# Banded attention and a gated feed-forward network on one core: another order for the loads, the transposes and the first feed-forward tile

## The chip, the core and the metric

The kernel runs on one core of a Trainium2 chip. Its engines run side by side, each through its own list of instructions in a fixed order: TensorE (PE, with its weight loads as PEld), VectorE (DVE), ScalarE (ACT), GpSimd (POOL) and SyncE (SP). The metric is the device time of one execution in microseconds (us); the time given is the median of the runs shown. An execution taken with the profiler gives the trace.

## The reference

Inputs q, k and v have 8 batches, 8 heads, 576 positions and 64 channels per head. Heads 0 to 3 use a plain window, heads 4 to 7 a dilated one:

```python
rel = pos[:, None] - pos[None, :]
mask_plain = (rel >= 0) & (rel < 32)
mask_dil   = (rel >= 0) & (rel < 128) & (rel % 4 == 0)
scores = where(mask, q @ k.T / 8, -1e9)
attn   = softmax(scores) @ v
x      = attn, heads side by side          # 4608 tokens x 512
out    = (((x @ w1) * (x @ w2)) @ w3) @ w_out   # w1, w2: 512x1024; w3: 1024x1024; w_out: 1024x512
```

## The kernel before, in words

**Attention.** The work of one batch is four steps: for each half of the positions (`hf`, 288 positions) one for the plain heads (`u` = 0) and one for the dilated heads (`u` = 1). A step computes scores on TensorE in two parts (L250), exponentials on ScalarE (L262), the product with a mask on VectorE (L264), the products with V on TensorE (L287), a reciprocal and a scaling on VectorE (L297, L298), and transposes into the channel-major activation `XT` (`to_channels`, L311 and L318), copied by VectorE for `u` = 0 (L326) and by ScalarE for `u` = 1 (L328). The operands come from `qn` and `kn` by transposes on VectorE (`transpose_qk`: into `qt` at L223, into `kt` at L212 or L223), V for the plain heads straight from memory (`vp`), and V for the dilated heads from a staging tile `vst` that a copy spreads into `vd` (`spread_vd`, two copies, L139). In the names of buffers qt0 and kt0 stand for `u` = 0, qt1 and kt1 for `u` = 1.

**Feed-forward.** w3 and w_out are first multiplied into one matrix `wf` (`fuse_t`, `fuse_m`). Tokens are taken in 9 tiles of 512. `ffn1` computes one block of 128 columns of x@w1 and x@w2 (two groups of four matmuls, L394), copies the first to SBUF on ScalarE (L404) and multiplies the second by it on VectorE (L405) into `gt`. Three PSUM banks `f` serve these groups in turn, so the third group ahead waits for the product before it. `ffn2` multiplies by `wf` (L429). Tile 0 is computed in two parts, tokens 0 to 287 and 288 to 511, since the first part needs only the first half of batch 0.

**Order.** Everything is issued by one hand-written sequence. The attention is a list of small pieces, `phases`; the feed-forward calls `point()` before each group, and a table `marks` says how many phases must have been issued by which point. Phases up to `done_at[1]` come before the first feed-forward group. `done_at[n]` is the place in the list at which step n has reached `XT`; the steps of batch b are 4b to 4b + 3. Inside the list the spread of V and the transposes for the next batch stand between the steps of the batch before it.

**Loads.** All loads are issued by GpSimd in program order, eight at most under way: the ninth issue waits for the first to land, and so on. They convert from float32 to bfloat16 on the way. The order is: batch 0 (q, k, vp, vst), w1 and w2, batch 1, w_out, w3 in four pieces, then batches 2 to 7, each issued by `prefetch` in the middle of the steps two batches ahead of it.

Of the kernel before, what the change touches and what calls it, by code (L numbers as in the profile page):

```python
# [22 lines left out]
HALF = 288  # L23
# [4 lines left out]
TB = 512  # L28
# [6 lines left out]
def kernel(  # L35
# [11 lines left out]
    nc = tc.nc  # L47
    B, H, s_, d_ = q.shape
# [5 lines left out]
    KFF = d_ff // P  # L54
# [47 lines left out]
    def load_qk(b, split=False):  # L102
        for nm, dst, src in (("qn", qn, q), ("kn", kn, k)):
            dst[b] = qk_pool.tile([P, 2, ROWS * D], BF16, tag=nm, name=nm)
        for u in range(2) if split else (slice(0, 2),):
            for dst, src in ((qn, q), (kn, k)):
                x = src[b].rearrange("(u h) (j a) d -> (h j) u (a d)", u=2, a=ROWS)
                nc.gpsimd.dma_start(out=dst[b][:, u], in_=x[:, u])  # L108

    def load_vp(b):  # L110
        vp = vps[b % NV]
        base = v[b, 0]

        def rows(p0, n, j0, nj):
            return bass.AP(
                tensor=base.tensor,
                offset=base.offset + (96 * j0 - 32 + p0) * D,
                ap=[[D, n], [96 * D, nj], [1, D]],
            )

        if b == 0:
            nc.gpsimd.dma_start(out=vp[32:P, 0:1, 0:D], in_=rows(32, 96, 0, 1))
            nc.gpsimd.dma_start(out=vp[:, 1:24, 0:D], in_=rows(0, P, 1, 23))
        else:
            nc.gpsimd.dma_start(out=vp[:, :, 0:D], in_=rows(0, P, 0, 24))

    def load_vd(b):
        vst[b] = qk_pool.tile([P, 2, 4, 4 * D], BF16, tag="vst", name="vst")
        for w in range(2):
            nc.gpsimd.dma_start(  # L130
                out=vst[b][:, w, :, :],
                in_=v[b, 4:8, 64 * w : 64 * w + 512, :].rearrange(
                    "h (p r) d -> p h (r d)", r=4
                ),
            )

    def spread_vd(b):
        for w in range(2):
            nc.vector.tensor_copy(  # L139
                out=vds[b % 2][:, w, :, 0:D],  # L140
                in_=vst[b][:, w, :, :].rearrange("p h (r d) -> p (h r) d", r=4),
            )
# [37 lines left out]
    def const_pool():  # L180
        def keep(t, base, pattern, cm):
            nc.gpsimd.affine_select(
                out=t, in_=t, compare_op=AL.is_ge, fill=0.0,
                base=base, pattern=pattern, channel_multiplier=cm,
            )

        mp = mp0.rearrange("p (r i) -> p r i", r=4)
        keep(mp, 32, [[1, 4], [4, 24]], -1)
        keep(mp, -1, [[-1, 4], [-4, 24]], 1)
        keep(md0, 0, [[56, 2], [1, RES]], -1)  # L190
        keep(md0, 31, [[-56, 2], [-1, RES]], 1)
        make_identity(nc, ident, nomemset=True)
# [12 lines left out]
    def transpose_qk(b, u, which):  # L205


        src, dst = ((qn, qts), (kn, kts))[which]
        t = src[b][:, u, :].bitcast(U32).rearrange("p (a i) -> p a i", a=ROWS)
        o = dst[u][b % 2].rearrange("p s c -> p (s c)").bitcast(U32)  # L210
        if u == 0 and which == 1:
            nc.vector.transpose(  # L212
                out=o[:, PADK : PADK + S].rearrange("p (j a) -> p a j", a=ROWS), in_=t
            )
            return
        for odd in range(2):
            n = 5 - odd
            step = (2 * 144 + 4, 5 - 2 * 144)[odd]
            first = o[:, 2 * 144 * odd : 2 * 144 * odd + 1]
            pitch = first.ap[0]  # L220
            for a1 in range(2):
                a0 = 2 * odd + a1
                nc.vector.transpose(  # L223
                    out=bass.AP(
                        tensor=first.tensor,
                        offset=first.offset + 144 * a1,
                        ap=[pitch, [1, n], [9, 16], [step, 2]],
                    ),
                    in_=t[:, a0 : a0 + 4 * n - 3 : 4, :],
                )  # L230

    class Step:
# [98 lines left out]

    early = [True]
    steps = [
        Step(4 * b + 2 * hf + u, b, u, hf)
        for b in range(B)
        for hf in range(2)
        for u in range(2)
    ]
    phases, done_at = [], {}
    issued = {0, 1}  # L340

    def prefetch(b):
        if b < B and b not in issued:
            issued.add(b)
            load_qk(b)
            load_vp(b)
            load_vd(b)

    def s_tile(hp):
        return ps_e if early[0] and hp else ps_s  # L350

    for i in range(len(steps) + 2):
        st = steps[i] if i < len(steps) else None
        p1 = steps[i - 1] if 1 <= i <= len(steps) else None
        p2 = steps[i - 2] if i >= 2 else None
        at = i % 4
        b = i // 4
        if st is not None and at == 0:
            phases.append(lambda b=b: transpose_qk(b, 1, 0))
        if at == 2 and b + 1 < B and st is not None:  # L360
            phases.append(lambda b=b: (spread_vd(b + 1), transpose_qk(b + 1, 0, 0)))
        if at == 3 and b + 1 < B and st is not None:
            phases.append(lambda b=b: transpose_qk(b + 1, 0, 1))
        if st is not None:
            phases.append(lambda st=st: st.scores(0, s_tile(0)))
        if p2 is not None:
            phases.append(lambda st=p2: st.to_channels())
            done_at[i - 2] = len(phases)
        if p1 is not None:
            phases.append(lambda st=p1: st.values(0))  # L370
        if st is not None and at == 0:
            phases.append(lambda b=b: transpose_qk(b, 1, 1))
            if b == 0:
                phases.append(lambda: spread_vd(0))
        if st is not None:
            phases.append(lambda st=st: st.scores(1, s_tile(1)))
        if p1 is not None and p1.u == 1:
            phases.append(lambda st=p1: st.values(1))
        if st is not None and at == 1:
            phases.append(lambda b=b: prefetch(b + 2))  # L380


    gts = {}
# [95 lines left out]
    load_wo()
    for g in range(4):  # L480
        load_w3(g)

    transpose_qk(0, 0, 0)
    transpose_qk(0, 0, 1)
    const_spread()
    n0 = done_at[1]
    for ph in phases[:n0]:
        ph()
# [2 lines left out]

    marks = [(0, n0), (14, done_at[3]), (29, done_at[7]), (69, done_at[11])]
    for t in range(3, 8):
        marks.append((72 + 24 * (t - 2) - 3, done_at[4 * t + 3]))
    xs, ys = [m[0] for m in marks], [m[1] for m in marks]
# [6 lines left out]
            phases[state[1]]()  # L504
            state[1] += 1

    for f in range(KFF):
        ffn1(0, f, point, 0, HALF)
    for f in range(KFF):
        ffn1(0, f, point, HALF, TB)  # L510
    for f in range(KFF):
        ffn1(1, f, point)
    fuse_t(0)
# [44 lines left out]
```

## Time and profile before

| | |
|---|---|
| median of the 3 runs shown | 322.04 us (319.61 to 322.6) |
| the profiled execution, its own time | 322.75 us |
| span in its trace | 321.1 us |
| TensorE busy in the span | 266.6 us (83%) |
| VectorE busy | 182.7 us (57%) |
| ScalarE busy | 122.0 us (38%) |
| GpSimd busy | 44.6 us (14%) |

The busy shares are means over the whole span. Idle time of an engine is given with what ended it; a number at a row's start is a time in us from the start of the span.

### The profile page before, as it was taken

The numbers are of one execution on the slowest core, as the hardware profiler recorded it, in microseconds if no ns is written. First come the engines' busy times: TensorE is split into PE (matmuls) and PEld (weight loads), VectorE is DVE, ScalarE is ACT, GpSimd is POOL, SyncE is SP. The second block draws the span as 40 slices with busy tenths as digits, with TensorE's granted clock in tenths as the row PEclk, the third lists the DMA queues.
The fourth block names the chain that finished last, engine by engine and source line by source line (L and its number), as shares of the span: only waits on it lengthen the run. The fifth ranks groups of instructions, "written<-read, shape, count | busy, mean of one in ns | idle before, by whom it ended". The sixth has DMA issues, their size and how long they took to land.

```text
span 321.1 us, 6289 instructions
## 1 busy us (share of the span) xinstructions
PE 266.6 (83%) x2586; PEld 144.1 (45%) x2624; DVE 182.7 (57%) x401; ACT 122.0 (38%) x205; POOL 44.6 (14%) x61
## 2 busy tenths in 40 slices
PE   0230089567997989999999999999999999999994
PEld 0130057445643545554545555545554554444441
DVE  4530388489674546478787787877775453132210
ACT  1220035324435343454535444454453542323332
POOL 8741414102200004000400400000000000000000
PEclk9999999859899899999999999999999999999999
DMA  7999999995910044923991892111111112111124
GB/s 121 176 210 198 200 212 209 192 181 82 169 22 2 0 77 69 205 80 54 167 145 34 143 191 63 35 35 44 56 35 33 35 46 55 47 53 56 44 65 131
DMA packets 47645, 31.86 MB, mean 99 GB/s; under 512 B 26624, under 2 KB 37888, under 8 KB 47616
## 3 DMA queue, kind: packets, MB, share of 16 engines
q0 software_dynamic: 41760, 22.02, 52.0%
q1 hardware_dynamic: 5856, 9.44, 10.0%
q8 instruction: 20, 0.33, 0.4%
q14 instruction: 9, 0.07, 0.1%
HBM read 44.03 MB, written 9.44 MB: 167 GB/s over the span
## 4 chain that ended last, share of the span: by engine, by line
PE 73%; DMA 16%; DVE 3%; POOL 3%; issue 1%; ACT 1%; POOLq 0%; ACTq 0%
PE f L394 36%; PE f L429 20%; DMA w3n<-in_moe_w_dram 7%; PE ps_s L250 6%; DMA vst<-in_v_dram 6%; PE f L459 5%; DMA w_sb<-in_moe_w_dram 4%; PE ps_o L287 4%; PE ps_x L318 1%; PE ps_x L445 1%; PE ps_x L311 1%; ACT w3T L451 1%; DVE xo L298 1%; DVE qt L223 1%; POOL vst L130 0%
## 5 line engine op out<-in xcount | busy, mean ns | idle before, releaser
L394 PE MATMUL f<-XT,w_sb 128*128 128x512 bf16 (+2 forms) x617 | 144.0, 366 | 1.3 <-issue 0.3
L394 PEld LDWEIGHTS <-w_sb 128*128 128x128 bf16 x640 | 57.7, 100 | 50.2
L405 DVE TENSOR_TENSOR gt<-f,asb 128x512 bf16<-128x512 f32 (+2 forms) x80 | 50.5, 631 | 42.6 <-PE f L394 38.7
L429 PE MATMUL f<-wf_sb,gt 128*128 128x512 bf16 x277 | 68.1, 380 | 0.6
L262 ACT ACTIVATE et<-ps_s 128x576 bf16<-128x576 f32 x61 | 39.8, 653 | 65.6 <-PE ps_s L250 65.4
L404 ACT CAST asb<-f 128x512 bf16<-128x512 f32 (+2 forms) x80 | 43.4, 542 | 51.8 <-PE f L394 50.6
L437 ACT COPY osb<-f 128x512 f32<-128x512 f32 x36 | 21.1, 585 | 53.8 <-PE f L429 50.4
L287 PEld LDWEIGHTS <-et 128*128 128x128 bf16 x448 | 21.9, 104 | 40.1 <-issue 28.3
L250 PE MATMUL ps_s<-qt,kt 32*128 32x72 bf16 (+1 forms) x856 | 29.0, 206 | 12.4 <-DVE kt L212 8.6
L429 PEld LDWEIGHTS <-gt 128*128 128x128 bf16 x288 | 25.8, 98 | 27.9
L298 DVE TENSOR_TENSOR xo<-ps_o,rcp 72x512 bf16<-72x512 f32 (+1 forms) x48 | 37.2, 775 | 1.7
L250 PEld LDWEIGHTS <-kt 32*128 32x128 bf16 x896 | 21.0, 99 | 35.3 <-issue 19.1
L287 PE MATMUL ps_o<-vd,et 128*128 128x65 bf16 x256 | 13.6, 198 | 26.8 <-DVE xo L298 26.8
L223 DVE STREAM_TRANSPOSE qt<-qn 128x160 uint32<-128x160 uint32 (+1 forms) x64 | 24.6, 422 | 4.5 <-DMA qn<-in_q_dram 3.4
L264 DVE TENSOR_TENSOR et<-et,mask_di 128x576 bf16<-128x576 bf16 x32 | 14.5, 455 | 15.3 <-ACT et L262 14.3
L264 DVE TENSOR_TENSOR et<-et,mask_pl 128x576 bf16<-128x576 bf16 x32 | 14.3, 447 | 12.8 <-ACT et L262 12.8
L139 DVE COPY vd<-vst 128x1024 bf16<-128x1024 bf16 x16 | 6.5, 434 | 25.1 <-DMA vst<-in_v_dram 25.1
L297 DVE RECIPROCAL rcp<-ps_o 72x8 f32<-72x8 f32 (+1 forms) x48 | 9.9, 207 | 18.4 <-PE ps_o L287 17.8
L108 POOL DMA_DIRECT2D qn<-in_q_dram x9 | 6.2, 687 | 93.0 <-DVE qt L223 43.1
L459 PE MATMUL f<-wo_sb,w3T 128*128 128x512 bf16 x60 | 16.6, 405 | 0.2
L287 PE MATMUL ps_o<-vp,et 128*128 128x65 bf16 x192 | 10.4, 209 | 4.1 <-DVE et L264 3.3
L130 POOL DMA_DIRECT2D vst<-in_v_dram x16 | 12.1, 762 | 7.3 <-DVE xo L298 3.4
(41 smaller groups left out, 130.5 us busy)
## 6 DMA issues: line engine op xcount, KB each, us to landing
out_dram<-osb SPq DMA_DIRECT2D x32, 144.0 KB
vst<-in_v_dram POOLq DMA_DIRECT2D x16, 256.0 KB, 9.9
qn<-in_q_dram POOLq DMA_DIRECT2D x7, 576.0 KB, 8.2
kn<-in_k_dram POOLq DMA_DIRECT2D x7, 576.0 KB, 7.2
vp<-in_v_dram POOLq DMA_DIRECT2D x7, 384.0 KB, 9.4
w3n<-in_moe_w_dram POOLq DMA_DIRECT2D x4, 512.0 KB, 20.4
w_sb<-in_moe_w_dram POOLq DMA_DIRECT2D x2, 768.0 KB, 14.2
wo_sb<-in_moe_w_out_dram POOLq DMA_DIRECT2D x1, 1024.0 KB, 23.0
```

The source lines that it names most:

```text
L223: nc.vector.transpose(out=bass.AP(tensor=first.tensor, offset=first.offset + 144 * a1, ap=[pitch, [1, n], [9, 16], [step, 2]],), in_=t[:, ...
L250: nc.tensor.matmul(out=sp[:, g, i * nq : (i + 1) * nq], lhsT=kt[prt, k0 : k0 + P, c], rhs=rhs[:, q0 : q0 + nq, c] if u else rhs.rearrange( ...
L262: nc.scalar.activation(out=ev, in_=sp[:, :, 0:HALF], func=ACT.Exp, scale=scale)
L264: nc.vector.tensor_tensor(out=ev, in0=ev, in1=mk.unsqueeze(1).to_broadcast([P, 2, HALF]), op=AL.mult)
L287: nc.tensor.matmul(out=ps_o[:, hp, j * (D + 1) : (j + 1) * (D + 1)], lhsT=self.et[:, c0 : c0 + P], rhs=rhs, start=True, stop=True,)
L298: nc.vector.tensor_tensor(out=xo[0:nq, :, 0:j, :], in0=ov[:, :, :, 0:D], in1=rcp[0:nq, :, 0:j].unsqueeze(3).to_broadcast([nq, 2, j, D]), o ...
L394: nc.tensor.matmul(out=ps, lhsT=w_sb[:, c, f * P : (f + 1) * P], rhs=XT[:, c, t0 + lo : t0 + hi], start=(c == 0), stop=(c == DCH - 1),)
L404: nc.scalar.copy(out=a_sb[:, 0 : hi - lo], in_=ps)
L405: nc.vector.tensor_tensor(out=gts[t][:, f, lo:hi], in0=pss[1], in1=a_sb[:, 0 : hi - lo], op=AL.mult)
L429: nc.tensor.matmul(out=y, lhsT=gts[t][:, f, tb * P : (tb + 1) * P], rhs=wf_sb[:, f, :], start=(f == 0), stop=(f == KFF - 1),)
L437: nc.scalar.copy(out=o_sb, in_=y)
L459: nc.tensor.matmul(out=ps, lhsT=w3T[ft][:, g, :], rhs=wo_sb[:, g, :], start=(g == 0), stop=(g == KFF - 1),)
```

## The change

The order of the loads, of the attention steps and of the first feed-forward tile is rewritten. The instructions are the same, but for where the first spread of V runs and how the first loads of w1 and w2 are cut.

- Steps of `u` = 1 come before steps of `u` = 0 in each half, and the transposes follow that order: for the next batch the `u` = 1 transposes stand between the steps of the batch before, and its `u` = 0 transposes at its own first step. The spread of the next batch moves from the third step (ahead of the q transposes) to the fourth (behind the k transposes).
- The phases of batch 0 are a list of their own; nothing of batch 1 stands in it. Batch 1 starts with its `u` = 1 transposes and its spread.
- vst is loaded ahead of vp. w1 and w2 are loaded in halves of 512 columns, the first half ahead of batch 1, the second behind it.
- The feed-forward of tile 0 goes by four blocks at a time: both parts of the tokens for blocks 0 to 3, then for blocks 4 to 7.
- The spread of batch 0 is done by ScalarE.

```diff
 def load_qk(b, split=False):
-        for u in range(2) if split else (slice(0, 2),):
+        for u in (1, 0) if split else (slice(0, 2),):
...
 def spread_vd(b):
         for w in range(2):
-            nc.vector.tensor_copy(
+            copy = nc.vector.tensor_copy if b else nc.scalar.copy
+            copy(
                 out=vds[b % 2][:, w, :, 0:D],
...
     steps = [
-        Step(4 * b + 2 * hf + u, b, u, hf)
+        Step(4 * b + 2 * hf + 1 - u, b, u, hf)
         for b in range(B)
         for hf in range(2)
-        for u in range(2)
+        for u in (1, 0)
     ]
...
-        if st is not None and at == 0:
-            phases.append(lambda b=b: transpose_qk(b, 1, 0))
-        if at == 2 and b + 1 < B and st is not None:
-            phases.append(lambda b=b: (spread_vd(b + 1), transpose_qk(b + 1, 0, 0)))
-        if at == 3 and b + 1 < B and st is not None:
-            phases.append(lambda b=b: transpose_qk(b + 1, 0, 1))
...
+    def segment(lo, hi):
+        for i in range(lo, hi + 2):
...
+            if i == lo:
+                phases.append(lambda b=b: transpose_qk(b, 1, 0))
+                phases.append(lambda b=b: transpose_qk(b, 1, 1))
+                if lo:
+                    phases.append(lambda b=b: spread_vd(b))
+            if st is not None:
+                if at == 0:
+                    phases.append(lambda b=b: transpose_qk(b, 0, 0))
+                if at == 2 and 4 * (b + 1) < hi:
+                    phases.append(lambda b=b: transpose_qk(b + 1, 1, 0))
+                if at == 3 and 4 * (b + 1) < hi:
+                    phases.append(lambda b=b: transpose_qk(b + 1, 1, 1))
+                phases.append(lambda st=st: st.scores(0, s_tile(0)))
...
+                if at == 3 and 4 * (b + 1) < hi:
+                    phases.append(lambda b=b: spread_vd(b + 1))
...
+    segment(0, 4)
+    segment(4, 4 * B)
...
-    marks = [(0, n0), (14, done_at[3]), (29, done_at[7]), (69, done_at[11])]
+    marks = [(0, n0), (8, done_at[3]), (16, done_at[3]), (30, done_at[7]), (69, done_at[11])]
...
-    for f in range(KFF):
-        ffn1(0, f, point, 0, HALF)
-    for f in range(KFF):
-        ffn1(0, f, point, HALF, TB)
+    for f4 in range(0, KFF, 4):
+        for lo, hi in ((0, HALF), (HALF, TB)):
+            for f in range(f4, f4 + 4):
+                ffn1(0, f, point, lo, hi)
```

What this does to the order on three engines:

GpSimd's issues from the first batch's last loads on, before (a row `x2` is two loads; `vst_134` is batch 0; `qn_141`, `kn_142`, `vp1_84` and `vst_146` are batch 1):

```order
L130 DMA vst_134<-in_v_dram 128x4x256 x2
L146 DMA w1_sb_75<-in_moe_w1_dram 128x4x256
L146 DMA w2_sb_76<-in_moe_w2_dram 128x4x256
L146 DMA w1_sb_75<-in_moe_w1_dram 128x4x768
L146 DMA w2_sb_76<-in_moe_w2_dram 128x4x768
L108 DMA qn_141<-in_q_dram 128x2x1152
L108 DMA kn_142<-in_k_dram 128x2x1152
L125 DMA vp1_84<-in_v_dram 128x24x64
L130 DMA vst_146<-in_v_dram 128x4x256 x2
L152 DMA wo_sb_77<-in_moe_w_out_dram 128x8x512
```

and now (`vst_132` and `vp0_83` are batch 0, `qn_139` to `vp1_84` batch 1):

```order
L123 DMA vp0_83<-in_v_dram 128x23x64
L147 DMA w1_sb_75<-in_moe_w1_dram 128x4x512
L147 DMA w2_sb_76<-in_moe_w2_dram 128x4x512
L108 DMA qn_139<-in_q_dram 128x2x1152
L108 DMA kn_140<-in_k_dram 128x2x1152
L130 DMA vst_143<-in_v_dram 128x4x256 x2
L125 DMA vp1_84<-in_v_dram 128x24x64
L147 DMA w1_sb_75<-in_moe_w1_dram 128x4x512
L147 DMA w2_sb_76<-in_moe_w2_dram 128x4x512
L153 DMA wo_sb_77<-in_moe_w_out_dram 128x8x512
```

Batch 1's four kinds of load stand ahead of the second half of w1 and w2, and within a batch vst stands ahead of vp; the loads that stand ahead of batch 2's q, up to the last piece of w3, are in sum those of before.

VectorE behind the first batch's transposes, before (`vst_134`, `qn_105`: batch 0; `vst_146`, `qn_141`: batch 1):

```order
L139 COPY vd0_86<-vst_134 128x16x64 x2
L264 TENSOR_TENSOR et0_88<-et0_88,mask_pl_81 128x576
L264 TENSOR_TENSOR et1_89<-et1_89,mask_di_82 128x576
L297 RECIPROCAL rcp_235<-ps_o_100 96x12
L298 TENSOR_TENSOR xo_222<-ps_o_100,rcp_235 96x768
L264 TENSOR_TENSOR et1_89<-et1_89,mask_di_82 128x576
L139 COPY vd1_87<-vst_146 128x16x64 x2
L223 STREAM_TRANSPOSE qt01_96<-qn_141 128x5x16x2 x2
L223 STREAM_TRANSPOSE qt01_96<-qn_141 128x4x16x2 x2
L264 TENSOR_TENSOR et2_90<-et2_90,mask_pl_81 128x576
```

and now:

```order
L265 TENSOR_TENSOR et0_88<-et0_88,mask_di_82 128x576
L213 STREAM_TRANSPOSE kt00_91<-kn_106 128x18x32
L265 TENSOR_TENSOR et0_88<-et0_88,mask_di_82 128x576
L265 TENSOR_TENSOR et1_89<-et1_89,mask_pl_81 128x576
L298 RECIPROCAL rcp_235<-ps_o_100 72x2x4
L299 TENSOR_TENSOR xo_226<-ps_o_100,rcp_235 72x2x256
L265 TENSOR_TENSOR et1_89<-et1_89,mask_pl_81 128x576
L298 RECIPROCAL rcp_261<-ps_o_100 72x2x4
L299 TENSOR_TENSOR xo_252<-ps_o_100,rcp_261 72x2x256
L265 TENSOR_TENSOR et2_90<-et2_90,mask_di_82 128x576
```

The copies from both vst tiles and the transposes of batch 1 are gone from this place: what follows the first step's masks is the attention of batch 0 alone. On ScalarE the copies stand ahead of the first exponentials now:

```order
L140 ACT_TABLE_LOAD
L140 COPY vd0_86<-vst_132 128x16x64 x2
L263 ACTIVATE et0_88<-ps_s_99 128x576
L263 ACTIVATE et0_88<-ps_e_102 128x576
L263 ACTIVATE et1_89<-ps_s_99 128x576
```

They wait for vst, and the exponentials of the first step queue behind them; before, the list began with the exponentials.

VectorE where the inputs of batch 2 are first needed, before (`vst_261`, `qn_256`: batch 2):

```order
L298 TENSOR_TENSOR xo_581<-ps_o_100,rcp_594 96x768
L264 TENSOR_TENSOR et2_90<-et2_90,mask_di_82 128x576
L139 COPY vd0_86<-vst_261 128x16x64 x2
L223 STREAM_TRANSPOSE qt00_95<-qn_256 128x5x16x2 x2
L223 STREAM_TRANSPOSE qt00_95<-qn_256 128x4x16x2 x2
L405 TENSOR_TENSOR gt_358<-f_636,asb_620 128x288
L264 TENSOR_TENSOR et0_88<-et0_88,mask_pl_81 128x576
L326 COPY XT_79<-ps_x_101 128x2x288
L297 RECIPROCAL rcp_679<-ps_o_100 72x2x4
```

and now (`qn_264`, `kn_265`, `vst_268`: batch 2):

```order
L298 RECIPROCAL rcp_659<-ps_o_100 72x2x4
L299 TENSOR_TENSOR xo_650<-ps_o_100,rcp_659 72x2x256
L224 STREAM_TRANSPOSE qt10_97<-qn_264 128x5x16x2 x2
L224 STREAM_TRANSPOSE qt10_97<-qn_264 128x4x16x2 x2
L265 TENSOR_TENSOR et0_88<-et0_88,mask_di_82 128x576
L415 TENSOR_TENSOR gt_355<-f_699,asb_675 128x288
L298 RECIPROCAL rcp_727<-ps_o_100 96x12
L299 TENSOR_TENSOR xo_714<-ps_o_100,rcp_727 96x768
L265 TENSOR_TENSOR et0_88<-et0_88,mask_di_82 128x576
L224 STREAM_TRANSPOSE kt10_93<-kn_265 128x5x16x2 x2
L224 STREAM_TRANSPOSE kt10_93<-kn_265 128x4x16x2 x2
L265 TENSOR_TENSOR et1_89<-et1_89,mask_pl_81 128x576
```

The first instructions of batch 2 were the copies from vst and are now the transposes of q; the copies stand behind the transposes of k, 18 instructions further down.

## Rows read from the trace of the kernel before

**Rows 1.** The page, 40 slices of the span (8.03 us each).

```profile
PEclk9999999859899899999999999999999999999999
DMA  7999999995910044923991892111111112111124
```

**Rows 2.** Stretches: us, busy time by engine (instructions), granted clock, DMA share, GB/s.

```profile
0.00:43.60 43.60, 7.75 (x151) 6.13 (x152) 17.04 (x53) 6.07 (x9) 21.96 (x35) 1.00 1.27 183
60.80:67.10 6.30, 0.03 (x1) 0.00 (x0) 4.14 (x12) 0.47 (x2) 0.00 (x0) 0.63 1.21 208
63.60:84.60 21.00, 15.27 (x213) 11.91 (x214) 17.51 (x45) 7.03 (x14) 4.35 (x5) 0.70 1.10 140
67.10:73.50 6.40, 6.32 (x88) 4.79 (x88) 5.12 (x12) 2.63 (x5) 0.00 (x0) 0.56 1.50 144
126.00:262.00 136.00, 134.44 (x1407) 69.05 (x1432) 97.40 (x205) 63.70 (x108) 10.10 (x12) 1.00 0.51 85
```

**Rows 3.** Timeline of VectorE: start, us, what [idle before <- what ended it].

```profile
17.11 0.44 DVE L264 TENSOR_TENSOR et<-et,mask_pl 128x576 bf16<-128x576 bf16 x1
...
36.16 0.43 DVE L139 COPY vd<-vst 128x1024 bf16<-128x1024 bf16 x1 [16.21 <-DMA vst<-in_v_dram]
...
39.27 0.44 DVE L264 TENSOR_TENSOR et<-et,mask_pl 128x576 bf16<-128x576 bf16 x1
...
61.91 0.43 DVE L139 COPY vd<-vst 128x1024 bf16<-128x1024 bf16 x1 [3.44 <-DMA vst<-in_v_dram]
63.28 0.43 DVE L139 COPY vd<-vst 128x1024 bf16<-128x1024 bf16 x1 [0.94 <-DMA vst<-in_v_dram]
63.62 1.60 DVE L223 STREAM_TRANSPOSE qt<-qn 128x160 uint32<-128x160 uint32 x4
...
84.22 0.38 DVE L405 TENSOR_TENSOR gt<-f,asb 128x224 bf16<-128x224 f32 x1
```

**Rows 4.** Timeline of TensorE, the same columns.

```profile
40.95 0.60 PE L287 MATMUL ps_o<-vd,et 128*128 128x65 bf16 x8 [19.77 <-DVE xo L298]
...
43.58 1.15 PE L394 MATMUL f<-XT,w_sb 128*128 128x288 bf16 x4
...
50.32 1.14 PE L394 MATMUL f<-XT,w_sb 128*128 128x288 bf16 x8
...
67.11 0.60 PE L287 MATMUL ps_o<-vd,et 128*128 128x65 bf16 x8 [6.28 <-DVE xo L298]
67.52 0.94 PE L394 MATMUL f<-XT,w_sb 128*128 128x224 bf16 x4
...
74.78 0.55 PE L394 MATMUL f<-XT,w_sb 128*128 128x224 bf16 x4
```

**Rows 5.** Timeline of GpSimd: the issues of the third batch's loads.

```profile
35.32 0.71 POOL L108 DMA_DIRECT2D qn<-in_q_dram  x1 [2.03 <-DMA vp<-in_v_dram]
36.67 0.72 POOL L108 DMA_DIRECT2D kn<-in_k_dram  x1 [0.64 <-DMA vst<-in_v_dram]
...
45.32 0.74 POOL L130 DMA_DIRECT2D vst<-in_v_dram  x1 [1.51 <-DMA w3n<-in_moe_w_dram]
```

**Rows 6.** Tile qn: time from issue to landing.

```profile
DMA to landing us min/median/max: 4.2/11.9/20.0
```

**Rows 7.** Tile kn: time from issue to landing.

```profile
DMA to landing us min/median/max: 5.3/11.4/21.4
```

**Rows 8.** VectorE, 63.6 to 84.6 us, by shape: busy us, mean ns | idle before.

```profile
L405 DVE TENSOR_TENSOR gt<-f,asb 128x224 bf16<-128x224 f32 x8 | 3.0, 375 | 0.0
L298 DVE TENSOR_TENSOR xo<-ps_o,rcp 72x512 bf16<-72x512 f32 x4 | 2.7, 687 | 0.1
...
L297 DVE RECIPROCAL rcp<-ps_o 72x8 f32<-72x8 f32 x4 | 0.8, 189 | 0.0
...
L139 DVE COPY vd<-vst 128x1024 bf16<-128x1024 bf16 x1 | 0.4, 427 | 0.9 <-DMA vst<-in_v_dram 0.9
```

**Rows 9.** Line 451, a ScalarE copy of 1024 elements: min/median/max ns.

```profile
L451 ACT COPY w3T<-ps_x x8: 1012/1012/1012, 100.5 to 121.6; 128x1024 bf16<-128x1024 bf16 x8
```

More of the change, by code (lines that the diff above doesn't have):

```diff
@@ L345, in prefetch @@
             load_qk(b)
+            load_vd(b)
             load_vp(b)
-            load_vd(b)
     def s_tile(hp):
         return ps_e if early[0] and hp else ps_s
[L352 to L357, printed above, removed]
-        if st is not None and at == 0:
-            phases.append(lambda b=b: transpose_qk(b, 1, 0))
-        if at == 2 and b + 1 < B and st is not None:
-            phases.append(lambda b=b: (spread_vd(b + 1), transpose_qk(b + 1, 0, 0)))
-        if at == 3 and b + 1 < B and st is not None:
-            phases.append(lambda b=b: transpose_qk(b + 1, 0, 1))
[L364 to L380, printed above, removed]
@@ new lines, in segment @@
+    def segment(lo, hi):
+        for i in range(lo, hi + 2):
+            st = steps[i] if i < hi else None
+            p1 = steps[i - 1] if lo <= i - 1 < hi else None
+            p2 = steps[i - 2] if lo <= i - 2 else None
+            at, b = i % 4, i // 4
+            if i == lo:
[11 more added lines that the diff above has]
+                phases.append(lambda st=st: st.scores(0, s_tile(0)))
+            if p2 is not None:
+                phases.append(lambda st=p2: st.to_channels())
+                done_at[i - 2] = len(phases)
+            if p1 is not None:
+                phases.append(lambda st=p1: st.values(0))
+            if st is not None:
+                if at == 0:
+                    phases.append(lambda b=b: transpose_qk(b, 0, 1))
+                if at == 3 and 4 * (b + 1) < hi:
+                    phases.append(lambda b=b: spread_vd(b + 1))
+                phases.append(lambda st=st: st.scores(1, s_tile(1)))
+            if p1 is not None and p1.u == 1:
+                phases.append(lambda st=p1: st.values(1))
+            if st is not None and at == 1:
+                phases.append(lambda b=b: prefetch(b + 2))
@@ L471 @@
     const_pool()
+    load_vd(0)
     load_vp(0)
-    load_vd(0)
-    load_w12(0, 256)
-    load_w12(256, 1024)
+    load_w12(0, 512)
     load_qk(1)
+    load_vd(1)
     load_vp(1)
-    load_vd(1)
+    load_w12(512, 1024)
     load_wo()
@@ L481 @@
         load_w3(g)
-    transpose_qk(0, 0, 0)
-    transpose_qk(0, 0, 1)
     const_spread()
+    spread_vd(0)
     n0 = done_at[1]
```

## The prediction

> **What bounds the kernel now.** I read the page's slices first. The 16 DMA engines are busy in nine tenths or more of each of the first nine slices, some 72 us, and hardly after [rows 1]; over the first 43.6 us they move 183 GB/s while TensorE works 7.75 us [rows 2]. So the start is a stretch of loading, and the question is what waits for which load. From 126 to 262 us TensorE works 134.44 of 136 us [rows 2]: there the kernel is at its limit, and the change does not touch it but for the order of the steps.
>
> The timeline of VectorE names the waits. It stands for 16.21 us until 36.16 for batch 1's vst, and from 58.47 to 61.91 and again until 63.28 for the two halves of batch 2's [rows 3]. TensorE stands 19.77 and 6.28 us behind these two [rows 4]. In each case the copy of the next batch's V is queued on VectorE ahead of masks and scalings of the batch at hand, which have all they need. The loads themselves are late because the queue in front of them is long: batch 2's last vst is issued at 45.32, when the first piece of w3 lands, and lands at 63.3 [rows 3, 5].
>
> **The first stall goes.** With nothing of batch 1 in the list of batch 0, the first feed-forward group no longer waits for batch 1. In before VectorE stood from 19.95 until its next mask at 39.27, and the first group came 4.3 us after that mask, at 43.58 [rows 3, 4]. Without the 19.3 us it would come at 24.3. Two things shift this. vst is now loaded ahead of vp, so it lands up to 2.7 us earlier (bounds 0 and 2.7). The two spreads run on ScalarE, and the exponentials of the first step queue behind them. No row has this copy on ScalarE: at least the 0.43 us of VectorE [rows 8], at most the 1.01 us of a ScalarE copy of as many elements [rows 9]; I take 1.01, the same engine and length. The exponentials, some 1.3 us, and two masks of 0.44 us follow. The second mask, which ended at 17.55 in before [rows 3], then ends between 16.5 and 19.5. I take a first group at 25 us, bounds 23 and 27: a head start of 18.6 us.
>
> The row on this copy says 1.01 against 0.43 us, so the move adds about 1.2 us ahead of the first exponentials. The Trainium skill, Perfetto Trace Analysis, section Optimizing Scalar/DVE Operations, says that where VectorE has a fast mode it does such an operation quicker, and that moving it to ScalarE makes sense when VectorE is saturated. VectorE works 17.04 of the first 43.6 us [rows 2], so by that rule the move is a loss: 314.2 us instead of 313.0 if it lay on the path; by the trace it lies under the wait told next.
>
> **But the second wait stays, at another load.** Batch 2's q and k come behind the same loads as before, in sum, up to the last of w3. In before qn is issued at 35.32 and the longest time to landing is 20.0 us, so it lands at 55.3; kn at 36.67 + 21.4 = 58.1 [rows 5 to 7]. With the DMA engines full throughout, an order among earlier loads cannot move this; I keep 55.3. The new first instruction of batch 2 on VectorE is the transpose of q, so this is where VectorE stands next. k follows at 58.1 and vst, now ahead of vp (about 2.7 us for its load), at about 60.6; the list reaches them later than that, so they cost nothing.
>
> Does VectorE arrive by 55.3? From the first group at 25: eight groups of the first part with the attention between them took 43.58 to 51.46, that is 7.9 us, in before [rows 4], and now the end of batch 0 hangs on it too: 8 to 10. Eight groups of 224 columns, 0.55 each [rows 4]: 4.4. Then on VectorE three sets of four transposes at 1.6 [rows 3], one long transpose, taken as a set too, two copies at 0.43, four masks at 0.44, two scalings with reciprocal at 0.88, two products at 0.4 [rows 3, 8]: 11.6, and 13.9 if it waits as much as in 63.6 to 84.6 (21.0 us for 17.5 of work) [rows 2]. Sum 49 to 53, with the bounds of the start 47 to 55. So it arrives first, and waits. The head start of 18.6 us is spent here: this is why the gain is far smaller than the stall that goes.
>
> **What comes after is compared with the same stretch of before.** From the first transposes of batch 2 at 63.62 to the last product of tile 0, ending at 84.6, VectorE took 21.0 us, 17.5 of it work [rows 2, 3]. By the order of the two programs the new stretch, from the transposes of batch 2's q to the last product of tile 0, has the same 13 transposes, 8 masks and 2 copies to XT; one scaling with reciprocal fewer (0.88), three products fewer (about 1.1), and two spreads more (0.85) [rows 8]. That is 1.1 us less: 19.9 us, if the waits stay at 3.5. The end of tile 0 comes at 55.3 + 19.9 = 75.2 instead of 84.6: 9.4 us. At that point eight matmuls on V are still to do that were done before, 0.4 us at TensorE's full clock. Gain **9.0 us**. Bounds: without any wait 16.4 us, a gain of 12.5; with an arrival 2 us late and twice the waits, a gain of 3.5.
>
> From there both programs run the same list against a busy TensorE, and batch 3's loads follow behind batch 2's: 2.1 MB at 208 GB/s [rows 2] are 10 us, so they are in by about 73.5, ahead of the end of tile 0, behind which their first use stands. Against the profiled execution this gives 322.75 - 9.0 = 313.75. That execution lies 0.71 above the median; the forecast for the median is 322.04 - 9.0 = **313.0 us**.
>
> **Rivals.**
> 1. *The head arrives late.* If the 47 to 55 of above is 58 to 61 because the new pieces wait on each other more than the old ones, every us past 55.3 is lost: 316 to 319, say 317. For it: the transposes and the spread of batch 1 now stand in one row with nothing between them, and TensorE has no mask to work on meanwhile. Against: the sum has up to 8 us to spare at its low end.
> 2. *TensorE's clock.* After the 6.3 us stall the granted clock is 0.56 from 67.1 to 73.5 us [rows 2], mostly the lower of its levels (1.2 of 2.4 GHz), and a group of 224 columns takes 0.94 us instead of 0.55 [rows 4]. In the new stretch TensorE has 9 groups and some 12 blocks of attention; at the lower clock 9 x 0.94 + 12 x 0.65 = 16.3 us from 57.7 (55.3 + 1.6 + 0.44 + 0.4), and 3.5 of waits: 77.5 instead of 75.2. If it is still low there, some 2 us more follow: 317.3. The Trainium skill, TensorE: Matmul & The Clock Gate, section HAM oscillation, says that a wait for a DMA between bursts of matmuls throttles the clock and the next burst starts cold; the trace agrees, with 0.56 behind the stall. By that rule this change, which keeps one stall, pays once, as before.
> 3. *Slower.* The clock stays low from the first group to the end of tile 0, because TensorE gets work only in short bursts between VectorE's. Price in the head: 13 groups of 288 columns at 1.15 instead of about 0.67, 6.2; 8 of 224 at 0.94 instead of 0.55, 3.1; 14 blocks of attention, 3.8; less the 2.2 that the start pays anyway: 10.9. VectorE then arrives at 60 to 65, about 8 late; with the 4.3 of rival 2 some 12.5 us are lost against 9.0 gained: 325.5. It turns to slower where more than 9.0 us are lost in all. Against it: in before the clock came back after the stall, to nine tenths or more in the slice from 72 to 80 us and to eight in the next [rows 1].
> 4. *The head start is kept.* If tile 0 ran on without batch 2, the end would move by 18.6 us: 303. Against it stands the transpose of batch 2's q inside the steps of batch 1.
>
> **How the numbers follow.** Forecast 0.62, rival 1 0.16, rival 2 0.13, rival 3 0.04, rival 4 0.05. The range: from the bound without waits, 309.5, and a little of a faster clock, 308.5, up to 319, which holds rivals 1 and 2; outside lie rivals 3 and 4 and a tenth of the rest. A measurement of this kernel tells about 1%, 3.2 us, from no change. Faster by more (under 318.8): forecast, rival 4 and most of 1 and 2, 0.86. Within 1%: the rest of 1 and 2, 0.10. Slower: rival 3, 0.04.
>
> **What would show it.** In the trace of the changed kernel: the first group of L404 (the old L394) at 23 to 27 us; batch 2's q landing at 55 to 56; VectorE's longest wait past 30 us standing before the transposes of that q, with a DMA as its end; the end of tile 0 at 73 to 78. Wrong would be a landing of q moved by more than 2 us, VectorE arriving after it, or more than 2 us of new idle time on TensorE after 126 us.

## The result, and the profile after

The changed kernel takes 309.61 us (median of 4 runs, 309.02 to 310.33) against 322.25 us for the kernel before (4 runs): a ratio of 0.9626 with a 95% interval of 0.957 to 0.9682. That is faster by 12.6 us, where 9.0 were forecast; the time lies inside the range of 308.5 to 319, near its low end. The profiled execution took 309.83 us, with a span of 308.1.

The page of the changed kernel, in 40 slices of 7.7 us:

```profile
PEclk9999966756999999999999999999999999999999
DMA  6999999999900249718916991111112111212124
```

In the first nine slices the loading is about as dense as before [rows 1]. The timeline of VectorE, where it stood for vst twice [rows 3]:

```profile
14.30 0.46 DVE L265 TENSOR_TENSOR et<-et,mask_di 128x576 bf16<-128x576 bf16 x1 [4.22 <-ACT et L263]
...
37.68 1.59 DVE L224 STREAM_TRANSPOSE qt<-qn 128x160 uint32<-128x160 uint32 x4
...
54.83 1.60 DVE L224 STREAM_TRANSPOSE qt<-qn 128x160 uint32<-128x160 uint32 x4 [5.65 <-DMA qn<-in_q_dram]
...
61.86 0.75 DVE L140 COPY vd<-vst 128x1024 bf16<-128x1024 bf16 x2
...
73.43 0.38 DVE L415 TENSOR_TENSOR gt<-f,asb 128x224 bf16<-128x224 f32 x1
```

The two stalls for vst are gone; the copies of batch 2's vst at 61.86 wait for nothing. One wait for a load is left past 30 us, the 5.65 us until 54.83, and what ends it is batch 2's q. VectorE stood there from 49.18. TensorE behind it, with the first feed-forward group at 24.37 instead of 43.58 and a stall of 4.06 us where there were 19.77 and 6.28 [rows 4]:

```profile
24.37 1.12 PE L404 MATMUL f<-XT,w_sb 128*128 128x288 bf16 x4 [0.42 <-DVE rcp L298]
...
40.31 0.24 PE L251 MATMUL ps_s<-qt,kt 32*128 32x72 bf16 x4 [2.56 <-DVE kt L224]
...
53.54 0.67 PE L404 MATMUL f<-XT,w_sb 128*128 128x288 bf16 x4
58.26 0.66 PE L312 MATMUL ps_x<-ident,xo 96*128 96x96 bf16 x6 [4.06 <-DVE xo L299]
...
59.17 0.94 PE L404 MATMUL f<-XT,w_sb 128*128 128x224 bf16 x4
```

The loads of batch 2's q and k, from GpSimd's timeline:

```profile
32.37 0.70 POOL L108 DMA_DIRECT2D qn<-in_q_dram  x1 [2.04 <-DVE xo L299]
34.90 0.71 POOL L108 DMA_DIRECT2D kn<-in_k_dram  x1 [1.83 <-DVE gt L415]
```

and the times from issue to landing of tile qn, whose longest is that of this q:

```profile
DMA to landing us min/median/max: 4.3/12.8/22.4
```

q is issued 3 us earlier than before and lands 22.4 us later, at 54.8: 0.5 us from where it landed before [rows 5, 6]. The stretch from there to the end of tile 0, by windows (columns as in [rows 2]):

```profile
54.83:73.81 18.98, 13.93 (x157) 10.12 (x159) 16.34 (x41) 5.29 (x10) 6.49 (x7) 0.58 1.56 193
90.26:111.91 21.65, 19.94 (x205) 11.71 (x208) 12.69 (x24) 9.95 (x11) 0.70 (x1) 1.00 0.18 29
```

The granted clock was 0.58 in it, lower than the 0.70 of the stretch of before [rows 2], and VectorE worked 16.34 of 18.98 us. The clock was low twice in tile 0: 0.54 from 40.31 to 51.39, behind the 2.56 us in which TensorE waited for batch 1's transposes, and 0.50 from 58.26 to 73.81, behind the 4.06 us; in between, from 51.39 to 54.21, it was 1.00.

The last row is a stage that the prediction did not price by itself, where w3 is multiplied by w_out. In the kernel before it ran from 99.82 to 125.50:

```profile
99.82:103.24 3.42, 1.22 (x17) 0.97 (x16) 0.69 (x1) 2.02 (x2) 0.00 (x0) 1.00 0.02 5
103.24:107.00 3.76, 3.76 (x27) 1.97 (x27) 0.83 (x2) 0.64 (x1) 0.00 (x0) 0.55 0.00 0
99.82:125.50 25.68, 22.11 (x208) 12.63 (x211) 12.62 (x26) 10.68 (x12) 2.46 (x3) 0.93 0.18 26
```

25.68 us there, 21.65 now. On TensorE, two of the attention's transposes (`to_channels`) stood there for ScalarE to empty the PSUM tile ps_x, which they share with the transposes of w3:

```profile
103.24 0.49 PE L318 MATMUL ps_x<-ident,xo 72*128 72x72 bf16 x8 [1.10 <-ACT w3T L451]
...
116.48 0.41 PE L311 MATMUL ps_x<-ident,xo 96*128 96x96 bf16 x6 [1.16 <-ACT w3T L451]
```

Now one does, and for less:

```profile
106.03 0.42 PE L319 MATMUL ps_x<-ident,xo 72*128 72x72 bf16 x8 [0.29 <-ACT w3T L461]
```

The table puts these places side by side, with those of the experiments told below (from the timelines, all in us; the differences in the text are taken from these columns, and each row is one execution). One of the four runs of e8 was in a slower state and is left out of its time below.

| kernel | first group of tile 0 | end of tile 0 | first transposes of w3 | first `ffn2` | span |
|---|---|---|---|---|---|
| before | 43.58 | 84.60 | 99.82 | 125.50 | 321.1 |
| the change | 24.37 | 73.81 | 90.26 | 111.91 | 308.1 |
| e1, spread on VectorE | 27.58 | 73.05 | 89.06 | 110.71 | 307.2 |
| e2, old load order | 26.70 | 74.23 | 89.45 | 111.11 | 307.9 |
| e3, one list | 29.05 | 74.16 | 89.39 | 111.04 | 307.4 |
| e4, batch 2 before w3 | 24.68 | 68.46 | 84.26 | 105.91 | 302.1 |
| e5, before + late spread | 34.78 | 75.87 | 91.72 | 113.36 | 308.9 |
| e6, mark 71 | 24.81 | 73.77 | 89.50 | 113.05 | 309.7 |
| e7, e4 + less on VectorE | 24.28 | 66.70 | 81.93 | 103.58 | 299.8 |
| e8, before + batch 2 before w3 | 43.06 | 77.51 | 92.79 | 118.47 | 314.0 |
| e9, before + mark 67 | 42.99 | 83.33 | 99.07 | 121.18 | 316.3 |
| e10, e7 + one list | 27.63 | 64.92 | 80.93 | 102.58 | 299.5 |
| e11, e5 + batch 2 before w3 | 34.19 | 69.86 | 85.77 | 107.40 | 303.0 |

So the 13.0 us of the span come as 10.8 up to the end of tile 0, 1.2 given back in tile 1, 4.0 in the stage of w3, and 0.6 given back after it.

### The profile page after: what moved, and what is told of

It reads as the page before. It is cut to its first block, busy times and chain, and to the rows that moved or that the text cites. A ratio compares the mean times of both kernels' runs of the same rounds, so it can differ in the third digit from the quotient of the medians.

```text
span 308.1 us, 6288 instructions
## 1 busy us (share of the span) xinstructions
PE 271.4 (88%) x2585; PEld 147.0 (48%) x2624; DVE 183.0 (59%) x399; ACT 124.7 (40%) x207; POOL 44.5 (14%) x61
## 4 chain that ended last, share of the span: by engine, by line
PE 77%; DMA 9%; DVE 7%; issue 2%; ACT 2%; POOL 1%; POOLq 0%; ACTq 0%
PE f L404 38%; PE f L439 20%; DMA qn<-in_q_dram 7%; PE ps_s L251 6%; PE f L469 4%; PE ps_o L288 4%; DMA vst<-in_v_dram 2%; DVE xo L299 2%; PE ps_x L319 1%; PE ps_x L312 1%; PE ps_x L455 1%; DVE qt L224 1%; DVE et L265 1%; DVE kt L213 1%; ACT w3T L461 1%
## 5 line engine op out<-in xcount | busy, mean ns | idle before, releaser
L404 PE MATMUL f<-XT,w_sb 128*128 128x512 bf16 (+2 forms) x621 | 147.9, 375 | 1.8 <-issue 0.5
L404 PEld LDWEIGHTS <-w_sb 128*128 128x128 bf16 x640 | 59.1, 102 | 52.2 <-issue 1.4
L251 PE MATMUL ps_s<-qt,kt 32*128 32x72 bf16 (+1 forms) x852 | 30.4, 212 | 20.5 <-DVE kt L224 11.0
L251 PEld LDWEIGHTS <-kt 32*128 32x128 bf16 x896 | 22.0, 102 | 43.5 <-issue 20.3
L288 PE MATMUL ps_o<-vd,et 128*128 128x65 bf16 x256 | 15.1, 208 | 1.4 <-DVE xo L299 1.4
L469 PE MATMUL f<-wo_sb,w3T 128*128 128x512 bf16 x60 | 15.1, 379 | 0.3 <-issue 0.2
L224 DVE STREAM_TRANSPOSE kt<-kn 128x160 uint32<-128x160 uint32 (+1 forms) x32 | 12.3, 420 | 0.6
L312 PE MATMUL ps_x<-ident,xo 96*128 96x96 bf16 x96 | 7.5, 219 | 5.8 <-DVE xo L299 5.3
```

The lines of the kernel that those rows point to most:

```text
L224: nc.vector.transpose(out=bass.AP(tensor=first.tensor, offset=first.offset + 144 * a1, ap=[pitch, [1, n], [9, 16], [step, 2]],), in_=t[:, ...
L251: nc.tensor.matmul(out=sp[:, g, i * nq : (i + 1) * nq], lhsT=kt[prt, k0 : k0 + P, c], rhs=rhs[:, q0 : q0 + nq, c] if u else rhs.rearrange( ...
L288: nc.tensor.matmul(out=ps_o[:, hp, j * (D + 1) : (j + 1) * (D + 1)], lhsT=self.et[:, c0 : c0 + P], rhs=rhs, start=True, stop=True,)
L404: nc.tensor.matmul(out=ps, lhsT=w_sb[:, c, f * P : (f + 1) * P], rhs=XT[:, c, t0 + lo : t0 + hi], start=(c == 0), stop=(c == DCH - 1),)
L469: nc.tensor.matmul(out=ps, lhsT=w3T[ft][:, g, :], rhs=wo_sb[:, g, :], start=(g == 0), stop=(g == KFF - 1),)
```

## The experiments

Theory 1 is the prediction's: up to the end of tile 0 the time is set by the load that VectorE's list asks for first, batch 2's q, and the 19 us by which the feed-forward starts earlier are worth only as much as is needed to be there when it lands. The rival is that the head start itself is the gain. Theory 2 is that the 4.0 us in the stage of w3 come from where the attention's pieces fall among the transposes of w3. Theory 3 is that VectorE's list bounds the stretch behind the landing, and TensorE's clock does not.

**e1: the spread of batch 0 back on VectorE.**

```diff
-            copy = nc.vector.tensor_copy if b else nc.scalar.copy
+            copy = nc.vector.tensor_copy
```

> The changed kernel with batch 0's spread of V back on VectorE, where it now stands ahead of the first transposes and waits for vst (11.3 and 12.7 us in the changed kernel's trace). The first feed-forward group then comes some 3 us later than 24.4. Theory 1 (VectorE has to be at batch 2's q by the time this lands, 54.8 us, and has 5.65 us to spare): no change, 309 to 310.3 us. Rival (the gain is the head start itself, every us of it counts): 3 us slower, 312 to 313.

309.22 us, ratio 0.9618 (0.9592 to 0.9645): no difference from the change. VectorE's timeline:

```profile
11.49 0.52 DVE L140 COPY vd<-vst 128x1024 bf16<-128x1024 bf16 x1 [6.08 <-DMA vst<-in_v_dram]
...
54.87 1.62 DVE L224 STREAM_TRANSPOSE qt<-qn 128x160 uint32<-128x160 uint32 x4 [3.11 <-DMA qn<-in_q_dram]
```

The first group came at 27.58, 3.2 us later, and the wait for q shrank from 5.65 to 3.11 us; it ended at the same time. This is what theory 1 says, and the rival's 3 us are not there. ScalarE's part of the change is worth nothing here.

**e2: the loads in the old order.**

```diff
-    load_vd(0)
     load_vp(0)
-    load_w12(0, 512)
+    load_vd(0)
+    load_w12(0, 256)
+    load_w12(256, 1024)
     load_qk(1)
-    load_vd(1)
     load_vp(1)
-    load_w12(512, 1024)
+    load_vd(1)
...
             load_qk(b)
-            load_vd(b)
             load_vp(b)
+            load_vd(b)
```

> The changed kernel with the loads in the order and the cuts of before (vp ahead of vst, all of w1 and w2 ahead of batch 1); steps, lists and tile 0 as changed. vst of batch 0 lands some 4 us later (16.6 instead of 12.7), batch 1's at 36 to 37.5. Theory 1: the start is 3 to 4 us later, inside the 5.65 us to spare; batch 2's vst lands behind its vp, at 63.3, where VectorE came for it at 61.9, so 1 us is lost: 310 to 311.5. Rival (head start counts): 313 to 314.

309.94 us, 0.9636 (0.9616 to 0.9655): just under the 310 to 311.5 that theory 1 gave, and not to be told from the change. The first group came 2.3 us later, where 3 to 4 were expected. VectorE's timeline:

```profile
54.90 1.61 DVE L224 STREAM_TRANSPOSE qt<-qn 128x160 uint32<-128x160 uint32 x4 [4.00 <-DMA qn<-in_q_dram]
...
62.77 0.43 DVE L140 COPY vd<-vst 128x1024 bf16<-128x1024 bf16 x1 [0.42 <-DMA vst<-in_v_dram]
```

q at 54.90 as before; only at vst, behind vp again, there is a wait of 0.42 us. The order of the loads, the first thing that the change is named for, is worth nothing measurable as long as the same 2 MB of w3 stand ahead of batch 2.

**e3: one list of steps for all batches.**

```diff
-    segment(0, 4)
-    segment(4, 4 * B)
+    segment(0, 4 * B)
```

> The changed kernel with one list of steps for all batches, so that batch 1's transposes and spread stand between the steps of batch 0 again and VectorE waits there for batch 1's loads (24 to 30 us). First feed-forward group 7 to 9 us later than 24.4. Theory 1: VectorE has 5.6 us less to do later and still reaches batch 2's q before 54.8: 309 to 311. Rival (head start counts): 316 to 318.

309.03 us, 0.9616 (0.9587 to 0.9645): no difference.

```profile
23.30 1.61 DVE L224 STREAM_TRANSPOSE qt<-qn 128x160 uint32<-128x160 uint32 x4 [2.80 <-DMA qn<-in_q_dram]
...
54.78 1.61 DVE L224 STREAM_TRANSPOSE qt<-qn 128x160 uint32<-128x160 uint32 x4 [8.58 <-DMA qn<-in_q_dram]
```

VectorE waits 2.80 us for batch 1's q between the steps of batch 0. The first group comes at 29.05, 4.7 us later than in the change where 7 to 9 were expected, and then VectorE is at batch 2's q earlier than in the change (46.20 against 49.18) and waits 8.58 us. The times that the rival gave for the three runs, 312 to 313, 313 to 314 and 316 to 318, did not come.

**e4: batch 2 loaded ahead of w3.**

```diff
     load_wo()
-    for g in range(4):
-        load_w3(g)
...
             load_vd(b)
             load_vp(b)
+            if b == 2:
+                for g in range(4):
+                    load_w3(g)
```

> The changed kernel with the loads of w3 (2 MB, some 10.5 us of the DMA engines) moved behind batch 2's loads; w3 is first needed at about 85 us. Theory 1: batch 2's q lands at about 44, VectorE's wait of 5.65 us before it goes, TensorE's clock does not fall for it: 301 to 304.5. Rival (the landing of batch 2 is not what sets the time, the work of the head is): 309 to 310.

303.8 us, 0.9443 (0.9408 to 0.9479). Where VectorE waited 5.65 us the rows now follow each other without a wait:

```profile
48.74 0.69 DVE L299 TENSOR_TENSOR xo<-ps_o,rcp 72x512 bf16<-72x512 f32 x1
49.34 1.60 DVE L224 STREAM_TRANSPOSE qt<-qn 128x160 uint32<-128x160 uint32 x4
```

The end of tile 0 came 5.35 us earlier, the span is 6.0 us shorter. Theory 1 stands: the landing of q was the bound, and the price of being late is nearly one to one (5.35 us for a wait of 5.65). TensorE's clock in the stretch, by windows:

```profile
49.34:68.46 19.12, 13.94 (x235) 10.44 (x236) 16.52 (x42) 8.38 (x16) 6.51 (x8) 0.87 1.29 204
```

0.87 instead of 0.58, and the stretch took 19.12 us against 18.98. That does not price the clock, for the two do not hold the same work: 235 matmuls here against 157, and 16 instructions on ScalarE against 10, since what these engines did in the change while VectorE waited falls into the stretch here. The runs of the changed kernel that wait for q are nearer to each other. From the end of that wait to the end of tile 0 their windows give:

| kernel | stretch, us | granted clock | matmuls | VectorE's work, us |
|---|---|---|---|---|
| e6 | 18.98 | 0.55 | 158 | 16.34 |
| the change | 18.98 | 0.58 | 157 | 16.34 |
| e2 | 19.33 | 0.65 | 177 | 16.45 |
| e1 | 18.18 | 0.72 | 173 | 16.32 |
| e3 | 19.38 | 0.73 | 176 | 16.92 |

The length does not follow the clock between 0.55 and 0.73. What a full clock would make of it no run shows.

**e5: the kernel before, with the spread of the next batch moved alone.**

```diff
-            phases.append(lambda b=b: (spread_vd(b + 1), transpose_qk(b + 1, 0, 0)))
+            phases.append(lambda b=b: transpose_qk(b + 1, 0, 0))
...
+        if at == 3 and b + 1 < B and st is not None:
+            phases.append(lambda b=b: spread_vd(b + 1))
         if st is not None:
             phases.append(lambda st=st: st.scores(1, s_tile(1)))
```

> The kernel before with one thing changed: the spread of the next batch's V stands behind the transposes of k, in the fourth step of the batch, instead of ahead of those of q in the third. Theory 1: VectorE's second wait is then for batch 2's q (55) instead of its vst (63.3), and it has less to wait for at the first one too; end of tile 0 at 76 to 78 instead of 84.6: 313 to 316. Rival (the split list, the load order or the order within tile 0 is needed): 319 to 322.

311.16 us, 0.9659 (0.963 to 0.9689): better than either side expected, 11.1 us where the whole change gave 12.6, with one spread moved. VectorE's timeline:

```profile
29.01 1.61 DVE L223 STREAM_TRANSPOSE qt<-qn 128x160 uint32<-128x160 uint32 x4 [10.61 <-DMA qn<-in_q_dram]
...
36.98 0.43 DVE L139 COPY vd<-vst 128x1024 bf16<-128x1024 bf16 x1 [0.36 <-DMA vst<-in_v_dram]
...
54.77 1.60 DVE L223 STREAM_TRANSPOSE qt<-qn 128x160 uint32<-128x160 uint32 x4 [5.54 <-DMA qn<-in_q_dram]
```

At the first stall it now waits for batch 1's q, 7 us ahead of its vst, and at the second for batch 2's q, at 54.77 as in all of these runs. The end of tile 0 came at 75.87, just ahead of the 76 to 78 expected. The 2 us by which the time is under the expected 313 to 316 were not in that sum: the stage of w3 is 21.64 us long here, as in the change, and so 4.0 us shorter than before.

**e6: the changed kernel with a mark moved.**

```diff
-    marks = [(0, n0), (8, done_at[3]), (16, done_at[3]), (30, done_at[7]), (69, done_at[11])]
+    marks = [(0, n0), (8, done_at[3]), (16, done_at[3]), (30, done_at[7]), (71, done_at[11])]
```

> The changed kernel with the mark 69 of the feed-forward set to 71, so that a to_channels stands right between two transposes of w3 on the one PSUM tile ps_x, twice, as it did in the kernel before; nothing else. Theory 2 (4 us of the gain come from the stage in which w3 is multiplied by w_out, where that pattern cost two waits of 1.1 to 1.2 us and 3.4 us at the lower clock): 2 to 4 us slower than the changed kernel, 311.5 to 313.5. Rival (those 4 us come from elsewhere, for one from an earlier landing): no change, 309 to 310.

311.75 us, 0.9677 (0.9638 to 0.9715). By its time alone it is not clear of the change; the rows of the stage decide. TensorE's timeline:

```profile
91.21 0.61 PE L455 MATMUL ps_x<-ident,w3n 128*128 128x128 bf16 x8 [1.10 <-ACT w3T L461]
92.92 0.41 PE L312 MATMUL ps_x<-ident,xo 96*128 96x96 bf16 x6 [1.10 <-ACT w3T L461]
...
108.97 0.42 PE L319 MATMUL ps_x<-ident,xo 72*128 72x72 bf16 x8 [1.16 <-ACT w3T L461]
```

Two to_channels wait for ScalarE to empty ps_x, 1.10 and 1.16 us, as in the kernel before; in the change one waits 0.29. The stage took 23.55 us instead of 21.65. So 1.9 of its 4.0 us are these handovers. The other 2.1 go with the clock, by comparison and not by a run of its own: it was 0.93 over the stage before and is 1.00 here. The clock did not fall here (1.00 in the window from 92.92 to 97), although the waits at its start are those of the kernel before, which ran at 0.55 behind them. What else has to come together for that stays open.

**e9: the kernel before with a mark moved.**

```diff
-    marks = [(0, n0), (14, done_at[3]), (29, done_at[7]), (69, done_at[11])]
+    marks = [(0, n0), (14, done_at[3]), (29, done_at[7]), (67, done_at[11])]
```

> The kernel before with the mark 69 of the feed-forward set to 67, so that no to_channels stands directly between two transposes of w3 on ps_x; nothing else. Theory 2: the two handovers of ps_x go (1.9 us by the run with mark 71), and if the fall of the clock in that stage hangs on them, 1.7 us more: 318.5 to 320.3. Rival: 321.5 to 322.5.

318.22 us, 0.9892 (0.9847 to 0.9937), some 4 us faster than before for one number (2 to 5 by the interval), and a little better than the 318.5 to 320.3 that theory 2 gave. The stage took 22.11 us instead of 25.68, at a granted clock of 1.00. Its to_channels on TensorE:

```profile
100.78 0.61 PE L445 MATMUL ps_x<-ident,w3n 128*128 128x128 bf16 x8 [1.10 <-ACT w3T L451]
...
110.38 0.41 PE L311 MATMUL ps_x<-ident,xo 96*128 96x96 bf16 x6 [0.29 <-ACT w3T L451]
```

The wait of 0.29 us is that of the changed kernel. A moved mark also changes how much of the attention falls into the stage, but that is not what sets its length: this one holds 214 matmuls against 208 before and is shorter, and that of e6 holds 200 against 205 in the change and is longer. Theory 2 stands: the stage's gain has to do with where the attention's pieces fall among the transposes of w3, and the change got it by the way, since the pieces in its list stand elsewhere.

**e7: e4 with less work on VectorE** (the edit of e4 is not shown again).

```diff
-            copy = nc.vector.tensor_copy if b else nc.scalar.copy
+            copy = nc.vector.tensor_copy if b > 2 else nc.scalar.copy
...
-            if self.u == 0:
+            if self.u == 0 and self.b > 1:
                 nc.vector.tensor_copy(out=dst, in_=xv)
             else:
                 nc.scalar.copy(out=dst, in_=xv)
```

> The run with batch 2 loaded ahead of w3, and the spreads of batches 1 and 2 and the plain heads' copies to XT of batches 0 and 1 moved from VectorE to ScalarE (about 2.8 us of VectorE's work between 23 and 69 us, 2.0 of it past 37.7). Theory 3 (VectorE's list bounds the stretch up to the end of tile 0, and TensorE's clock does not): end of tile 0 some 1.5 to 2 us earlier, 301.5 to 302.5 against 303.8. Rival (latencies from engine to engine, or the clock, bound it): 303.5 to 304.5.

302.62 us, 0.9407 (0.9368 to 0.9446), between what theory 3 and its rival gave: the median is 1.2 us under e4's, with intervals that overlap; the end of tile 0 is 1.76 us earlier. But not as theory 3 has it. Windows, from batch 2's first transposes to the end of tile 0:

```profile
47.13:66.70 19.57, 14.09 (x246) 10.83 (x246) 15.30 (x38) 11.59 (x21) 7.23 (x9) 0.89 1.33 204
```

VectorE worked 15.30 us in it instead of 16.52, and the stretch took 19.57 instead of 19.12. All of the gain was made ahead of it, by coming to the transposes 2.2 us earlier. Theory 3 falls for the stretch: 1.2 us less work on VectorE did not shorten it. Four copies now stand on ScalarE instead, which worked 11.59 us in it against 8.38. That the chain from engine to engine sets its length is what is left, but it was not tested by itself.

**e8: the kernel before with batch 2 loaded ahead of w3** (the edit of e4 on the kernel before).

> The kernel before with only the loads of w3 moved behind batch 2's. Theory 1: batch 2's vst lands at about 53, ahead of VectorE, which came for it at 58.5; the second wait goes, 5 us: 315.5 to 317.5. Rival (the second wait is not on the path): 321 to 322.

315.71 us (median of three runs, 315.03 to 318.36), 0.982 (0.9762 to 0.9878): a gain of 4 to 8 us by the interval, where theory 1 gave 315.5 to 317.5 and the rival 321 to 322. VectorE comes to batch 2's vst at 56.85, and does not wait:

```profile
35.56 0.43 DVE L139 COPY vd<-vst 128x1024 bf16<-128x1024 bf16 x1 [17.09 <-DMA vst<-in_v_dram]
...
56.85 0.75 DVE L139 COPY vd<-vst 128x1024 bf16<-128x1024 bf16 x2
```

The second stall was on the path, as theory 1 has it; the first, for batch 1's vst, is untouched.

**e11: the kernel before with the edits of e5 and e8.**

> The kernel before with two edits: the spread of the next batch behind the transposes of k, and w3 loaded behind batch 2. Theory 1: of the 5.54 us that VectorE waited for batch 2's q with the first edit alone all but the arrival goes: 305 to 306.5. Rival (split list, load order and tile 0's order count as soon as that wait is gone): 308 to 311.

305.0 us, 0.9485 (0.9422 to 0.9547): at the low end of the 305 to 306.5 that theory 1 gave, faster than the whole change, and not to be told from e4, which is the whole change with w3 loaded later. VectorE's timeline:

```profile
28.43 1.60 DVE L223 STREAM_TRANSPOSE qt<-qn 128x160 uint32<-128x160 uint32 x4 [10.01 <-DMA qn<-in_q_dram]
...
49.01 1.62 DVE L223 STREAM_TRANSPOSE qt<-qn 128x160 uint32<-128x160 uint32 x4
```

It waits 10.01 us for batch 1's q, and not at all for batch 2's.

**e10: everything, with one list** (e7 with the edit of e3).

> The run with batch 2 ahead of w3 and less on VectorE, with one list of steps instead of a list of its own for batch 0. In the run with one list VectorE was at batch 2's q 3 us earlier (46.2 instead of 49.2) and then waited 8.58 us for it; with batch 2 ahead of w3 it lands before that. Theory 1 and 3: the 3 us are kept, 298.5 to 301. Rival (the split list is worth something by itself): 302.5 or more.

301.5 us, 0.9364 (0.9307 to 0.9421): the lowest median of all, but 0.5 us above the range of 298.5 to 301, and only 1.1 us under e7, with intervals that overlap. VectorE's timeline:

```profile
23.17 1.61 DVE L224 STREAM_TRANSPOSE qt<-qn 128x160 uint32<-128x160 uint32 x4 [2.84 <-DMA qn<-in_q_dram]
...
47.03 1.62 DVE L224 STREAM_TRANSPOSE qt<-qn 128x160 uint32<-128x160 uint32 x4
```

It was at batch 2's q at 47.03, against 47.13 in e7. The 3 us that I took from e3 were not kept, so this was a miss, and why is open. The end of tile 0 is still 1.8 us earlier, and the later stages give most of it back.

## Why the prediction was right

- **The bound.** That the wait for batch 2 would stay and move from its vst to its q is shown by the one wait left at 54.83, and by e1 to e3: the first group moved between 24.37 and 29.05, the end of the wait between 54.78 and 54.90, the time not at all. That it was the price is shown by e4, where the wait is gone and 5.35 us of it are gained. The prediction read its first rows loosely: the first of its nine slices shows 7, not 9, and the eleventh shows 9 again [rows 1]. Nothing in its sum hangs on that.
- **The head.** First group forecast at 25, measured 24.37. One bound was wrong: vst landed 3.9 us earlier than before (11.34 and 12.68), where I had allowed 2.7, and the second mask ended at 16.22, ahead of the 16.5 to 19.5 given. The copy on ScalarE took 1.05 us, where I had taken 1.01. Arrival at batch 2's q forecast at 49 to 53, measured 49.18. The move of the copy to ScalarE neither lost nor gained in the total (e1). Ahead of the wait it gained 3.2 us against e1, for the copy does not hold up the transposes that are queued behind it there on VectorE: the order of a list counted for more than the speed of the engine. The Trainium skill, Perfetto Trace Analysis, section Optimizing Scalar/DVE Operations, says that VectorE is faster at such an operation where it has a fast mode, and that offloading to ScalarE may make sense when VectorE is saturated. The trace agrees on the speed, 1.05 against 0.43 us; the loss that the prediction drew from it did not come.
- **The landing.** Forecast 55.3, measured 54.8.
- **The stretch behind it.** Forecast 19.9 us, measured 18.98; its end 73.81, where 73 to 78 was given. The count of instructions was right (16.34 us of work where 16.4 was counted); 2.6 us of waits came instead of 3.5.
- **What was given back.** 0.4 us were forecast for the matmuls that are still to do; tile 1 took 16.45 us instead of 15.22 (139 matmuls in it against 122), so it was 1.2.
- **The mis-sized term.** "From there both programs run the same list against a busy TensorE" was taken as zero. It holds behind the first `ffn2` (0.6 us; TensorE idle 6.96 us there against 6.12, under the 2 us that would have spoken against the prediction), not in the stage of w3, which gave 4.0 us. I had read the stage as part of a busy TensorE; its row says 22.11 of 25.68. In the spans, the terms of the sum gave 9.0 us without it: 10.8 where 9.4 were forecast, less 1.2 where 0.4 were, less 0.6 where nothing was. That they meet the 9.0 is in part luck, since their errors cancel, and that the table of marks gave 4.0 us more and not less was luck too.
- **The rivals.** Rival 1 did not come (5.65 us to spare). Rival 2's condition came and its price did not: the clock was 0.50 from 58.26 to the end of tile 0, but this came at 73.81, not at 77.5. The Trainium skill, TensorE: Matmul & The Clock Gate, section HAM oscillation, says that a wait for a DMA between bursts of matmuls throttles the clock. The trace agrees, with 1.00 ahead of the stall and 0.50 behind it. That the change pays once, as before, did not hold: the clock fell twice, the first time behind a stall of 2.56 us at batch 1's transposes, a place that the prediction names in rival 1 but not for the clock. So rival 3's condition came for 26.6 of the 49.4 us from the first group to the end of tile 0, without its price: VectorE was at the q at 49.18, where 60 to 65 was given. What the clock did cost is open. Rival 4 is ruled out by the wait for q, and by the end of tile 0, 10.8 us earlier and not 18.6.

## What to carry to other kernels

An engine's list is a queue: before a stall is priced, look for what stands behind the waiting instruction that has its inputs already, and for the next load that the same list will ask for, since that load's landing capped the gain here. A stall that hung on a full queue of loads was cured by the order of what stood ahead of it, not by starting the rest earlier: e11, one spread moved and w3 loaded later, beats the whole rewrite, and the spread alone (e5) comes within 1.6 us of it. And where pieces are spread among other work by a table, moving any number of them shifts their alignment everywhere behind; compare the stages that the change does not touch, too.

## What the runs showed of the hardware that was not expected

- In five runs a stretch of mixed attention and feed-forward, from the same wait on, took 18.18 to 19.38 us at granted clocks from 0.55 to 0.73, in no order of the clock.
- In the changed kernel the clock was 0.54 behind a stall of TensorE of 2.56 us, back at 1.00 some 11 us later, and 0.50 behind one of 4.06 us.
- Two waits of 1.10 us on one PSUM tile were followed by 3.8 us at a clock of 0.55 in the kernel before, and by 4.1 us at 1.00 in e6 with the same two waits. What decides was not found.
